# Attention scores as fp32 products on row halves of the array, decay and mask added on DVE

## The chip, the core and the metric

The kernel runs on one core of a Trainium2 chip. The core has TensorE (PE in the profile; its weight loads are PEld), the vector engine DVE, the scalar engine ACT, GpSimd (POOL), and SyncE (SP), whose queue starts the transfers. The metric is the device time of one execution in microseconds (us).

## The reference

Three parts follow one another: attention with a decay, a mixture of 8 experts whose gates are balanced by 8 rounds of scaling, and a two-layer part with a smooth activation. The change lies in the attention:

```python
scores = scale * np.matmul(q, k.transpose(0, 1, 3, 2))        # B=2, H=8, S=576, D=64
cum = np.cumsum(np.log(np.clip(f, 0.0001, 1.0)), axis=-1)
decay = cum[:, :, :, None] - cum[:, :, None, :]
scores = np.where(causal, -1000000000.0, scores + decay)
scores = scores - np.max(scores, axis=-1, keepdims=True)
attn = np.exp(scores)
attn = attn / (np.sum(attn, axis=-1, keepdims=True) + 1e-09)
return np.matmul(attn, v)
```

Its output x is the input of the experts (x @ w1, ReLU, @ w2, weighted by the gates), and theirs that of the last part.

## The kernel before

The order of all work is written out by hand, one loop of half steps `s`; each engine does its instructions in that order. Attention has ten query tiles, five a batch (`QT`: 128 queries, with one tile of 64 in each batch), with 128, 256, 384, 512 and 576 keys to look at. They are called tile 0 to tile 9 here; tiles 0 to 4 are batch 0, and tile 5 has the 64 queries of batch 1. A unit is a pair of heads of one tile, four units a tile, 40 in all; unit `pi` has the half steps `a` = 0 and 1, one for each of its heads.

A product of full precision is made from parts in the reduced type fp32r (FR): a value is a high part and a low part, each exact in that type. For the scores (`scores`, L361 on) the queries and keys of a tile are split into parts (`split`, L308, which calls `split2`, L284), turned by TensorE with head dimension on the partitions (`trans`, L321, 4 transposes a call, two calls each for queries and keys), and evacuated from PSUM by ACT or DVE, whichever the planner `pick` (L268) has given less time so far. `duplicate` (L300) copies half of the result by a transfer. A head's scores are two fp32r products that add up in PSUM: L374 with 128 rows, high and low query parts on the high key parts, and L375 with 96 rows, the missing product of parts and four rows that hold the decay (`cum_q`, `cum_k` load them). Scores of up to 512 keys are one group; 576 keys are two groups of 288. The mask pass on DVE (L387) adds a row of the mask, writes the negated scores and keeps their minimum; `expo` (L394) takes exponentials on ACT with their sums, one half step later; `normalize` (L402) multiplies by the reciprocal on POOL, `transposes` (L418) turns the weights in fp32, two units later, and `attend` (L444) multiplies them with v, three units later. In `attend` the two heads of a unit lie side by side on column halves of the array, 64 columns each; these are fp32 products.

Two other streams fill TensorE: `fill` (L535) takes the next piece of `filler` (L489), the first expert half on the tokens that are done, three products a piece, and `wsplit` (L565) splits its weights on ACT and DVE from unit 12 on. `warm` (L356) makes products without use that keep TensorE active in the first units. `gate` computes the gate logits of a chunk of 384 tokens. After the attention come the experts, from L695 on, with the same code in both kernels.

Of the kernel before, what the change touches and what calls it, by code (L numbers as in the profile page):

```python
# [8 lines left out]
F32 = mybir.dt.float32  # L9
# [74 lines left out]
def attention_moe_kernel(  # L84
# [46 lines left out]
    with ExitStack() as actx:  # L131
        ap1 = actx.enter_context(tc.tile_pool(name="ap1", bufs=1))
        rawp = actx.enter_context(tc.tile_pool(name="rawp", bufs=3))
        hlp = actx.enter_context(tc.tile_pool(name="hlp", bufs=2))
        kp = actx.enter_context(tc.tile_pool(name="kp", bufs=1))
        vp = actx.enter_context(tc.tile_pool(name="vp", bufs=6))
        pp = actx.enter_context(tc.tile_pool(name="pp", bufs=3))
        ptp = actx.enter_context(tc.tile_pool(name="ptp", bufs=2))
# [29 lines left out]
        cd = drp.tile([2, 16, S], F32, name="cd")  # L168


        KW = 832
        kbase = (256, 0)
        kt = kp.tile([128, H, KW], FR, name="kt")
        kbf = kp.tile([128, H, KW], FR, name="kb")
        kb = kbf[:96]
        qa = [kp.tile([128, 4, 128], FR, name=f"qa{i}") for i in range(3)]
        qb = [kp.tile([96, 4, 128], FR, name=f"qb{i}") for i in range(3)]

        def q_rows(i, engine=None):
            engine = engine or nc.gpsimd  # L180
            engine.memset(f(qb[i][64:96]), 0.0)
            engine.memset(f(qb[i][64:68]), -1.0)

        def k_rows(lo, hi, engine=None):
            (engine or nc.gpsimd).memset(f(kb[64:96, :, lo:hi]), 1.0)
# [17 lines left out]
        k_rows(256, 384, nc.vector)  # L203
        q_rows(0, nc.gpsimd)
        q_rows(1, nc.gpsimd)
        nc.vector.tensor_scalar(out=ft, in0=ft, scalar1=1e-4, scalar2=1.0, op0=ALU.max, op1=ALU.min)
        nc.vector.tensor_copy(out=idr, in_=idn)

        def cumulate(lo, hi, part=None):
            w = hi - lo  # L210
            if part != 1:
                cumulate_a(lo, hi, w)
            if part != 0:
                cumulate_b(lo, hi)

        def cumulate_a(lo, hi, w):
# [6 lines left out]
        def cumulate_b(lo, hi):  # L223
            nc.scalar.copy(out=chl[:, 0, lo:hi].bitcast(FR), in_=cum[:, lo:hi])
            nc.vector.tensor_tensor(
                out=chl[:, 1, lo:hi].bitcast(FR), in0=cum[:, lo:hi], in1=chl[:, 0, lo:hi], op=ALU.subtract
            )
            if lo == 0:
                for a in range(2):
# [1142 lines left out]
```

## Time and profile before

| | us |
|---|---|
| median of 3 runs | 1121.14 |
| lowest, highest | 1119.29, 1121.34 |
| span of the profiled execution, first to last instruction | 1123.8 |

The profiled execution has no time of its own beside its span; no run's time lies above it, so there is nothing around the span to add. Busy shares of its span are 99% for TensorE (with modelled ends), 76% for DVE, 45% for ACT and 7% for POOL. The engines' busy times are read by stretches below. "PEclk" is the granted share of TensorE's full clock: 1.0 is 2.4 GHz, 0.5 is 1.2 GHz, and a stretch with a value between had both.

### The profile page before, as it was taken

The page shows a single profiled execution, that of the slowest core. Times are in us where ns is not written, and L with a number is a line of the kernel's source. Part 1 is how long each engine was busy: PE and PEld are TensorE (multiplying, and loading weights), DVE is VectorE, ACT ScalarE, POOL GpSimd, SP SyncE. Part 2 cuts the span into 40 slices and gives each one's busy share as a digit, 9 for nine tenths or more (in the row PEclk, how much of TensorE's full clock was granted, in tenths as well). Part 3 has the DMA queues.
Part 4 walks back from the last instruction along what each step waited for, and adds up shares of the span by engine and source line. Part 5 has one row for each costly group of instructions (what it writes and reads, how often), then busy time and mean ns, then how long its engine had stood idle before and what let it go on. Part 6 is the DMA issues. An engine that isn't in the chain of part 4 may idle for free.

```text
span 1123.8 us, 17611 instructions
## 1 busy us (share of the span) xinstructions
PE 1109.8 (99%) x6608; PEld 981.3 (87%) x6608; DVE 852.3 (76%) x1850; ACT 504.3 (45%) x1128; POOL 76.7 (7%) x126
## 2 busy tenths in 40 slices
PE   8999999999999999999999999999999999999998
PEld 7677778989889898898988989899898988899996
DVE  7865655957786877868678686887868658998886
ACT  6766643245344253442534424243342335555554
POOL 5535420000000000000000000000000000000000
PEclk8899999999999999999999999999999999999999
DMA  5524212021332313323133241223311675000000
GB/s 124 145 65 105 53 39 76 20 75 42 128 110 77 124 50 130 105 75 132 49 113 110 86 140 58 94 96 111 122 67 57 205 253 198 1 29 1 29 1 29
DMA packets 78058, 98.93 MB, mean 88 GB/s; under 512 B 35190, under 2 KB 39046, under 8 KB 77974
## 3 DMA queue, kind: packets, MB, share of 16 engines
q1 hardware_dynamic: 77974, 97.81, 27.2%
q8 instruction: 52, 0.85, 0.3%
q14 instruction: 32, 0.26, 0.1%
HBM read 74.38 MB, written 19.21 MB: 83 GB/s over the span
## 4 chain that ended last, share of the span: by engine, by line
PE 93%; DVE 4%; ACT 1%; issue 1%; POOL 0%; DVEq 0%; ACTq 0%; POOLq 0%
PE pa L725 41%; PE pb L1080 28%; PE ph L695 11%; PE x L453 2%; PE pt L429 2%; PE pa L525 1%; PE sp L374 1%; PE ph L506 1%; PE pt L325 1%; DVE p L387 1%; PE sp L375 1%; PE x L862 0%; DVE r L973 0%; DVE r L967 0%; PE wt L359 0%
## 5 line engine op out<-in xcount | busy, mean ns | idle before, releaser
L725 PE MATMUL pa<-w2h,big 128*128 128x512 f32 x924 | 299.7, 393 | 1.2 <-DVE hid_b L703 1.2
L725 PEld LDWEIGHTS pa<-w2h,big 128*128 128x128 f32 x924 | 173.7, 188 | 39.7 <-DVE hid_b L703 1.5
L725 PE MATMUL pa<-w2l,big 128*128 128x512 f32 x528 | 207.2, 392 | 0.0
L1109 ACT COPY snap<-pb 128x288 f32<-128x288 f32 x168 | 66.4, 395 | 142.2 <-PE pb L1080 141.9
L725 PEld LDWEIGHTS pa<-w2l,big 128*128 128x128 f32 x528 | 99.3, 188 | 20.7
L703 DVE SCALAR_TENSOR_TENSOR big<-c,big 128x288 fp32r<-128x288 f32 x140 | 64.2, 459 | 69.4 <-ACT big L702 65.4
L702 ACT ACTIVATE big<-c 128x288 fp32r<-128x288 f32 x168 | 74.8, 445 | 91.8 <-DVE c L1114 89.0
L845 DVE SCALAR_TENSOR_TENSOR acc<-pa,P,acc 128x512 f32<-128x512 f32 x132 | 92.8, 746 | 27.2 <-PE pa L725 27.1
L1080 PE MATMUL pb<-xh,ss 128*128 128x288 f32 x448 | 103.9, 296 | 0.0
L1080 PE MATMUL pb<-tt,ss 128*128 128x288 f32 x672 | 103.7, 296 | 0.0
L1080 PEld LDWEIGHTS pb<-tt,ss 128*128 128x128 f32 x672 | 93.8, 188 | 1.0 <-ACT snap L1109 0.8
L1114 DVE TENSOR_TENSOR c<-pb,snap 128x288 f32<-128x288 f32 x168 | 75.9, 452 | 22.5 <-PE pb L1080 22.5
L824 ACT CAST db<-da 128x512 fp32r<-128x512 f32 x32 | 19.9, 621 | 147.8 <-DVE da L815 147.8
L1080 PEld LDWEIGHTS pb<-xh,ss 128*128 128x128 f32 x448 | 76.9, 188 | 0.6 <-DVE c L1114 0.3
L1080 PE MATMUL pb<-xl,ss 128*128 128x288 f32 x224 | 66.5, 297 | 0.0
L1080 PE MATMUL pb<-xh,w1l 128*128 128x288 f32 x224 | 66.2, 296 | 0.0
L1080 PE MATMUL pb<-xl,w1h 128*128 128x288 f32 x224 | 66.2, 295 | 0.0
L1080 PE MATMUL pb<-xh,w1h 128*128 128x288 f32 x224 | 66.1, 295 | 0.0
L725 PE MATMUL pa<-w2h,hid_b 128*128 128x512 f32 x150 | 58.6, 391 | 0.0
L397 ACT ACTIVATE p<-p,nmax 128x256 f32<-128x256 f32 (+6 forms) x80 | 48.4, 605 | 11.0 <-DVE nmax L387 8.4
L75 DVE TENSOR_TENSOR w2l<-stg,w2h 128x512 fp32r<-128x512 f32 x60 | 41.2, 690 | 15.9 <-ACT w2h L74 15.9
L413 POOL TENSOR_SCALAR p<-p,rs 128x256 f32<-128x256 f32 (+6 forms) x80 | 46.7, 596 | 66.4 <-DVE rs L409 42.2
(229 smaller groups left out, 2402.3 us busy)
## 6 DMA issues: line engine op xcount, KB each, us to landing
stg<-in_moe_w_dram SPq DMA_DIRECT2D x64, 512.0 KB
raw<-in_moe_w_in_dram SPq DMA_DIRECT2D x16, 512.0 KB
raw<-in_moe_w_out_dram SPq DMA_DIRECT2D x16, 512.0 KB
w_in_h<-db SPq DMA_DIRECT2D x16, 256.0 KB
w_in_l<-da SPq DMA_DIRECT2D x16, 256.0 KB
w_out_h<-db SPq DMA_DIRECT2D x16, 256.0 KB
w_out_l<-da SPq DMA_DIRECT2D x16, 256.0 KB
out_dram<-acc SPq DMA_DIRECT2D x9, 256.0 KB
```

What stands on the lines that cost most here:

```text
L75: (lo_engine or nc.vector).tensor_tensor(out=lo, in0=raw, in1=f(hi), op=ALU.subtract)
L397: nc.scalar.activation(out=p[:n, a, :nk], in_=p[:n, a, :nk], func=AF.Exp, bias=prev, scale=-1.0, accum_out=u["ssum"][:n, 0, a:a + 1],)
L413: nc.gpsimd.tensor_scalar(out=p[:n, a, :nk], in0=p[:n, a, :nk], scalar1=r[:n, a:a + 1], scalar2=1.0, op0=ALU.mult, op1=ALU.mult,)
L429: nc.tensor.transpose(out=pt[:, o + j * n:o + (j + 1) * n], in_=p[:n, a, j * 128:(j + 1) * 128], identity=idn[:n, :n],)
L695: nc.tensor.matmul(out=ph, lhsT=w[wn][kk][:, fs], rhs=x[c][:, kk], start=(kk == 0 and n == 0), stop=(kk == KD - 1 and n == 2),)
L702: nc.scalar.activation(out=hh, in_=ph, func=AF.Relu)
L703: nc.vector.scalar_tensor_tensor(out=hl, in0=ph, scalar=0.0, in1=f(hh), op0=ALU.max, op1=ALU.subtract)
L725: nc.tensor.matmul(out=pa, lhsT=a_[:, ts_], rhs=w[wn][ft_], start=(first and n == 0), stop=(last and n == 2),)
L845: nc.vector.scalar_tensor_tensor(out=acc[t], in0=pa, scalar=P[:, t, e:e + 1], in1=acc[t], op0=ALU.mult, op1=ALU.add)
L1080: nc.tensor.matmul(out=by_chunk(out_) if len(v_.shape) == 3 else out_, lhsT=u, rhs=v_, start=first and m == 0, stop=m == 5, skip_group_che ...
L1109: nc.scalar.copy(out=t, in_=bank["x", g])
L1114: nc.vector.tensor_tensor(out=t, in0=bank[of, g], in1=snap[with_, g], op=ALU.add)
```

## The change

Queries and keys stay unsplit in fp32. A transpose turns two heads at once, 64 rows of the array each (`turn`, 4 transposes for all 8 heads of queries or keys), so that a head's dimension lies on the upper or the lower 64 partitions. `scores` makes both heads of a unit together, at `a` = 0: a head is one fp32 product on its half of the array's rows; with 576 keys the last 64 or 128 keys are a further product each, in PSUM buffers of the transposes. The decay of the query is the same along a row and cancels, so it is left out; that of the keys is added on DVE, in fp32, by the pass that added the mask: `largest` has one pass over the keys before the tile's own (`bias`, loaded to all partitions by `load_bias`) and one over the tile's own keys (`diag`, loaded by `load_diag` and masked on POOL by `mask_diag`), the second continuing from the first one's minimum. For tile 0 that block comes from TensorE and DVE (`spread`). The products with v are made for two units at a time, at every second unit; `x_out` evacuates them. `duplicate`, `cum_q`, `cum_k`, the splits and their row fills are gone. The piece of `fill` moves from ahead of the products with v to the end of the half step. Two of the filler's hidden buffers come from the staging pool, whose buffers also take the expert weights. The diff, cut to its core:

```diff
-        rawp = actx.enter_context(tc.tile_pool(name="rawp", bufs=3))
-        hlp = actx.enter_context(tc.tile_pool(name="hlp", bufs=2))
+        rawp = actx.enter_context(tc.tile_pool(name="rawp", bufs=4))
         kp = actx.enter_context(tc.tile_pool(name="kp", bufs=1))
+        mdp = actx.enter_context(tc.tile_pool(name="mdp", bufs=2))
         vp = actx.enter_context(tc.tile_pool(name="vp", bufs=6))
         pp = actx.enter_context(tc.tile_pool(name="pp", bufs=3))
-        ptp = actx.enter_context(tc.tile_pool(name="ptp", bufs=2))
+        ptp = actx.enter_context(tc.tile_pool(name="ptp", bufs=3))
...
-        chl = pt0[1][:16, :, :S]
+        neg = pt0[1][:16, 0, :S]
         zer = ap1.tile([16, 1], F32, name="zer")
-        mask = ap1.tile([128, 704], F32, name="mask")
-
+        pick8 = ap1.tile([16, H, 128], F32, name="pick8")
+        mask = ap1.tile([128, 128], F32, name="mask")
...
+        cd = drp.tile([16, S], F32, name="cd")
+
+        KW = 704
+        kbase = (128, 0)
+        kt = kp.tile([128, 4, KW], F32, name="kt")
+        bias = kp.tile([128, H, KW], F32, name="bias")
+        hs1 = kp.tile([128, 12, 128], FR, name="hs1")
+        qt = [kp.tile([128, 4, 128], F32, name=f"qt{i}") for i in range(3)]
...
+        nc.gpsimd.memset(pick8, 0.0)
+        nc.gpsimd.affine_select(
+            out=pick8, in_=pick8, compare_op=ALU.not_equal, fill=-1.0, base=0,
+            pattern=[[-1, H], [0, 128]], channel_multiplier=1,
+        )
+        nc.gpsimd.memset(mask, 0.0)
+        nc.gpsimd.affine_select(
+            out=mask, in_=mask, compare_op=ALU.is_ge, fill=NEG, base=0,
+            pattern=[[-1, 128]], channel_multiplier=1,
...
+        def negate(lo, hi):
+            nc.scalar.mul(out=neg[:, lo:hi], in_=cum[:, lo:hi], mul=-1.0)
+            nc.sync.dma_start(out=cd[:, lo:hi], in_=neg[:, lo:hi])
+
+        def load_bias(b, lo, hi):
+            nc.sync.dma_start(
+                out=bias[:, :, kbase[b] + lo:kbase[b] + hi],
+                in_=cd[b * H:(b + 1) * H, lo:hi].partition_broadcast(128),
+            )
...
+        diag = {}
+
+        def span(b, i):
+            s0, n = QT[b][i]
+            return s0, min(S, -(-(s0 + n) // 128) * 128) - s0
+
+        def load_diag(ti):
+            b, i = tiles[ti]
+            s0, w = span(b, i)
+            diag[ti] = mdp.tile([128, H, 192], F32, tag="md", name="md")
+            nc.sync.dma_start(
+                out=diag[ti][:, :, :w], in_=cd[b * H:(b + 1) * H, s0:s0 + w].partition_broadcast(128)
+            )
+
+        def mask_diag(ti):
+            b, i = tiles[ti]
+            s0, w = span(b, i)
+            nc.gpsimd.affine_select(
+                out=diag[ti][:, :, :w], in_=diag[ti][:, :, :w], compare_op=ALU.is_ge, fill=NEG, base=0,
+                pattern=[[0, H], [-1, w]], channel_multiplier=1,
...
+        load_raw("q", q, 0, 128, 128)
+        load_raw("k", k, 0, 128, 128)
...
+        def turn(kind, ti, us=slice(0, 4)):
...
+            raw = raws[kind, b, s0]
+            pt = ps_t.tile([128, 4, 128], F32, tag="pt", name="pt")
+            for u in range(us.start, us.stop):
+                nc.tensor.transpose(
+                    out=pt[:, u, :n], in_=raw[:n, 2 * u:2 * u + 2].rearrange("p h d -> p (h d)"),
+                    identity=idn[:n, :n],
+                )
+            cols = (us.stop - us.start) * n
+            if kind == "q":
+                evac(qt[ti % 3][:, us, :n], pt[:, us, :n], cols, 0.125)
+            else:
+                o = kbase[b] + s0
+                evac(kt[:, us, o:o + n], pt[:, us, :n], cols)
...
-        def scores(u, a):
-            b, h, n, nk = u["b"], u["h"] + a, u["n"], u["nk"]
...
-            widths = [nk] if nk <= 512 else [nk // 2, nk // 2]
-            groups, o = [], 0
-            for w in widths:
...
+        def scores(u):
+            b, h, n, nk, s0 = u["b"], u["h"], u["n"], u["nk"], u["s0"]
+            k0, g = kbase[b], u["h"] // 2
+            lhs = [qt[u["ti"] % 3][64 * a:64 * a + 64, g, :n] for a in range(2)]
+            early = u["ti"] < 2 and g % 2
+            sp = [
+                (ps_f if early else ps_s).tile([128, 512], F32, tag="fb" if early else "s", name="sp")
+                for _ in range(2)
+            ]
+            rest = nk - s0 if nk > 512 else 0
+            if rest:
+                far = [ps_t.tile([128, 512], F32, tag="pt", name="far") for _ in range(2)]
+
+            def product(o, a, lo, hi):
+                nc.tensor.matmul(
+                    out=o, lhsT=lhs[a], rhs=kt[64 * a:64 * a + 64, g, k0 + lo:k0 + hi], start=True, stop=True
+                )
+
+            for a in range(2):
+                product(sp[a][:n, :nk - rest], a, 0, nk - rest)
+            if rest:
+                for a in range(2):
+                    product(far[a][:n, :rest], a, s0, nk)
+            u["p"] = pp.tile([128, 2, S], F32, tag="p", name="p")
+            u["ssum"] = sums4[(4 * u["ti"] + h // 2) % 4]
+            u["parts"] = []
+            for a in range(2):
+                parts = [(sp[a][:n, :s0], bias[:n, h + a, k0:k0 + s0], 0, s0)] if s0 else []
+                d = far[a][:n, :rest] if rest else sp[a][:n, s0:nk]
+                parts.append((d, diag[u["ti"]][:n, h + a, :nk - s0], s0, nk))
+                u["parts"].append(parts)
+
+        def largest(u, a):
+            n, p = u["n"], u["p"]
             prev = 3.0e38
-            for t, o, w in groups:
+            spent("dve", 110 + 67 + 1.05 * u["nk"])
+            for s_, t_, lo, hi in u["parts"][a]:
                 am = small.tile([128, 1], F32, tag="nmax", name="nmax")
                 nc.vector.tensor_tensor_reduce(
-                    out=p[:n, a, o:o + w], in0=t[:n, :w], in1=mask[:n, m0 + o:m0 + o + w],
-                    scale=-1.0, scalar=prev, op0=ALU.add, op1=ALU.min, accum_out=am[:n],
+                    out=p[:n, a, lo:hi], in0=s_, in1=t_, scale=-1.0, scalar=prev, op0=ALU.add, op1=ALU.min,
+                    accum_out=am[:n],
                 )
                 prev = am[:n]
             u["nmax", a] = prev
...
+        def x_out(u):
...
-                hs = []
-                for i in range(4):
-                    h0, c0 = 3 * (i % 2), 576 + 128 * (i // 2)
-                    hs.append(tuple(t[:, h0:h0 + 3, c0:c0 + 128] for t in (kt, kbf)))
+                hs = [tuple(hs1[:, 6 * i + 3 * j:6 * i + 3 * j + 3] for j in range(2)) for i in range(2)]
             for i in range(4):
+                if len(hs) == i:
+                    t = stage.tile([128, 2, 512], FR, tag="stg", name="spare")
+                    hs.append(tuple(t[:, j, :CH].rearrange("p (j t) -> p j t", j=3) for j in range(2)))
...
+        def spread(h0):
+            pb = ps_s.tile([128, 512], F32, tag="s", name="pb")
+            for h in range(4):
+                nc.tensor.matmul(
+                    out=pb[:, 128 * h:128 * h + 128], lhsT=pick8[:, h0 + h], rhs=cum[:, :128],
+                    start=True, stop=True,
+                )
+            nc.vector.tensor_tensor(
+                out=diag[0][:, h0:h0 + 4, :128], in0=pb.rearrange("p (h t) -> p h t", h=4),
+                in1=mask.unsqueeze(1).to_broadcast([128, 4, 128]), op=ALU.add,
+            )
+
+        def turn_half(g):
+            for kind in "qk":
+                turn(kind, 0, slice(2 * g, 2 * g + 2))
+
+        diag[0] = mdp.tile([128, H, 192], F32, tag="md", name="md")
+        cumulate(128, S)
         warm(8)
-        cumulate(128, S, 1)
+        turn_half(0)
+        spread(0)
         load_v(0, 0)
-        cum_k(0, 128, 256)
-
-        first = [
-            lambda: (qs0(1), ks0(1)), lambda: (qt0(1, True), kt0(1, True)),
-        ]
+        negate(0, S)
+        load_diag(1)
+        load_bias(0, 0, 128)
+        first = [lambda: spread(4), lambda: turn_half(1)]
...
             if live:
-                scores(units[pi], a)
+                if not a:
+                    scores(units[pi])
+                largest(units[pi], a)
             if s < 16:
                 warm(1)
-            fill()
-            if a and 3 <= pi < nu + 3:
-                w = units[pi - 3]
-                attend(w)
-                if w["h"] == H - 2 and w["ti"] in (2, 6, 9):
-                    c = (2, 6, 9).index(w["ti"])
-                    gates.append(c)
-                    if c < 2:
-                        fills.append(filler(c))
-                elif gates:
-                    logits.append(gate(gates.pop(0)))
-            elif logits:
+            if not a and pi % 2 == 0 and 4 <= pi < nu + 4:
+                for w in units[pi - 4:pi - 2]:
+                    attend(w)
+                if w["h"] == H - 2:
+                    x_out(w)
+                    if w["ti"] in (2, 6, 9):
+                        c = (2, 6, 9).index(w["ti"])
+                        gates.append(c)
+                        if c < 2:
+                            fills.append(filler(c))
+            elif a and gates:
...
                 if (st, a) == (0, 0):
-                    cum_q(nb_, ni, 0, (2 * ti + 2) % 3)
-                    qs()
+                    next_loads(ti + 2)
                 elif (st, a) == (0, 1):
-                    ks()
-                    next_loads(ti + 2)
-                elif (st, a) == (1, 0):
-                    qt_(0)
+                    turn("q", ti + 1)
                 elif (st, a) == (1, 1):
-                    kt_(0)
+                    turn("k", ti + 1)
                     load_v(nb_, ni)
-                elif (st, a) == (2, 0):
-                    qt_(1)
-                elif (st, a) == (2, 1):
-                    kt_(1)
-            if late_rows and s >= 2:
-                late_rows.pop(0)()
+                if (st, a) == (0, 1) and ti:
+                    load_diag(ti + 1)
+                    lo = [0, 0, 64, 192, 320][ni] if nb_ else 128 * max(ni - 1, 0)
+                    hi = [0, 64, 192, 320, 448][ni] if nb_ else 128 * ni
+                    if hi > lo:
+                        load_bias(nb_, lo, hi)
+                elif (st, a) == (3, 0):
+                    mask_diag(ti + 1)
+            fill()
```

## Rows read from the trace of the kernel before

**Rows 1.** Windows of attention and the rest: length, busy us (instructions) of engines, PEclk, DMA, GB/s.

```profile
0.00:178.00 178.00, 171.28 (x1346) 136.38 (x1346) 115.21 (x385) 112.11 (x287) 76.68 (x126) 0.94 0.37 87
178.00:1123.80 945.80, 938.52 (x5264) 844.92 (x5263) 737.12 (x1466) 392.23 (x841) 0.00 (x0) 1.00 0.26 88
```

**Rows 2.** Windows of the start, of tiles 0 to 3, and of tile 8.

```profile
core 0: us, PE busy (x) PEld busy (x) DVE busy (x) ACT busy (x) POOL busy (x), PEclk, DMA share, GB/s
0.00:9.50 9.50, 8.12 (x48) 7.93 (x48) 6.28 (x11) 4.23 (x9) 6.85 (x21) 1.00 0.32 72
9.50:21.80 12.30, 10.22 (x64) 9.22 (x64) 8.37 (x32) 9.64 (x28) 4.53 (x12) 0.72 0.76 161
21.80:31.40 9.60, 9.45 (x83) 7.88 (x82) 7.98 (x31) 8.16 (x26) 5.94 (x13) 1.00 0.63 142
31.40:42.00 10.60, 10.27 (x91) 7.79 (x89) 9.06 (x30) 8.73 (x23) 6.66 (x11) 1.00 0.80 203
42.00:64.80 22.80, 21.72 (x129) 15.76 (x128) 14.72 (x39) 12.57 (x33) 9.36 (x12) 0.70 0.34 88
...
124.40:142.00 17.60, 17.60 (x142) 14.45 (x141) 11.45 (x36) 12.16 (x30) 8.02 (x10) 1.00 0.23 55
```

**Rows 3.** The chain of waits by line, to 64.8 us and from there to 178.

```profile
by line: PE pt L429 11.4%; PE x L453 9.9%; PE sp L374 9.0%; PE pt L325 8.0%; PE sp L375 6.2%; PE wt L359 3.9%; issue 3.7%; DVE p L387 3.4%; PE ph L506 3.0%; DVE big L298 2.6%; ACT p L397 2.2%; DVE hl L288 2.1%; DVE hl L290 2.0%; POOL hl L29
...
by line: PE x L453 18.3%; PE pt L429 14.6%; PE pa L525 14.5%; PE ph L506 11.5%; PE sp L374 8.9%; DVE p L387 7.0%; PE sp L375 5.3%; PE pt L325 4.7%; issue 3.1%; DVE xl L460 1.5%; PE g L469 1.3%; PE g L474 1.2%; DVE qb L280 1.0%; PE pt L440 0
```

**Rows 4.** Timeline of TensorE's products: start us, duration us, line, tiles, shapes, count.

```profile
7.48 2.02 PE L359 MATMUL wt<-idn 128*128 128x128 f32 x16
...
21.27 0.44 PE L453 MATMUL x<-pT,v 128*64 128x128 f32 x4
...
42.57 0.39 PE L374 MATMUL sp<-kt,qa 128*128 128x512 f32 x1
42.80 0.39 PE L375 MATMUL sp<-kb,qb 96*128 96x512 f32 x1
43.12 0.88 PE L453 MATMUL x<-pT,v 128*64 128x128 f32 x12
43.93 0.88 PE L429 MATMUL pt<-idn,p 128*128 128x128 f32 x6
44.56 0.48 PE L374 MATMUL sp<-kt,qa 128*128 128x512 f32 x1
...
74.91 0.54 PE L325 MATMUL pt<-idr,hl 128*128 128x128 f32 x4
75.29 0.31 PE L374 MATMUL sp<-kt,qa 128*64 128x288 f32 x1
```

**Rows 5.** Groups by line and form in the attention: mask passes on DVE, an evacuation on ACT.

```profile
L387 DVE CUSTOM_DVE_ANT_0 p<-sp,mask 128x512 f32<-128x512 f32 x16 | 10.9, 685 | 7.0 <-PE sp L375 6.9
...
L387 DVE DVE_READ_ACCUMULATOR2_ANT nmax<- 128x1 f32 x72 | 5.9, 82 | 0.0
...
L387 DVE CUSTOM_DVE_ANT_0 p<-sp,mask 128x128 f32<-128x128 f32 x8 | 2.2, 280 | 0.5 <-PE sp L375 0.5
...
L276 ACT ACTIVATE qa<-pt 64x512 fp32r<-64x512 f32 x12 | 7.0, 586 | 5.7 <-PE pt L325 4.9 <-DVE qb L280 0.8
```

**Rows 6.** Groups by line on POOL in the attention.

```profile
L290 POOL TENSOR_TENSOR hl<-raw,hl 128x512 fp32r<-128x512 f32 (+1 forms) x14 | 18.4, 1315 | 13.5 <-PE sp L375 7.6 <-ACT hl L286 5.9
...
L242 POOL TENSOR_SCALAR_AFFINE_SELECT mask<-mask 128x704 f32<-128x704 f32 x1 | 0.8, 774 | 0.1
```

**Rows 7.** Timeline of the start, all engines.

```profile
4.29 0.70 ACT L318 CAST hl<-raw 128x256 fp32r<-128x256 f32 x2
...
9.54 0.30 PE L374 MATMUL sp<-kt,qa 128*128 128x128 f32 x1
...
11.04 0.27 DVE L387 CUSTOM_DVE_ANT_0 p<-sp,mask 128x128 f32<-128x128 f32 x1
```

**Rows 8.** Timeline in tile 3: POOL and DVE, and the next scores.

```profile
44.05 1.34 POOL L290 TENSOR_TENSOR hl<-raw,hl 64x512 fp32r<-64x512 f32 x1 [0.92 <-PE sp L375]
44.28 1.66 DVE L298 TENSOR_TENSOR big<-stg,big 128x512 fp32r<-128x512 f32 x1
46.85 0.51 PE L374 MATMUL sp<-kt,qa 128*128 128x512 f32 x1 [0.92 <-DVE nmax L387]
```

More of the change, by code (lines that the diff above doesn't have):

```diff
@@ L221, in cumulate_a @@
             )
[L223 to L226, printed above, removed]
-            )
-            if lo == 0:
-                for a in range(2):
-                    nc.sync.dma_start(
-                        out=f(kb[66 + a:67 + a, :, kbase[0]:kbase[0] + hi]), in_=chl[:H, a, :hi]
-                    )
-                    nc.sync.dma_start(out=f(qb[0][64 + a:65 + a, :, :hi]), in_=chl[:4, a, :hi])
-            nc.sync.dma_start(out=cd[:, :, lo:hi].rearrange("a p s -> p a s"), in_=chl[:, :, lo:hi])
@@ L236, in attention_moe_kernel @@
-        cumulate(0, 128)
-        early = stage.tile([128, 2, H, D], F32, tag="stg", name="early")
-        for a, (nm, src) in enumerate((("q", q), ("k", k))):
-            nc.sync.dma_start(out=early[:, a], in_=src[0, :, 128:256, :].rearrange("h p d -> p h d"))
-            raws[nm, 0, 128] = early[:, a]
-        nc.gpsimd.memset(mask, 0.0)
-        nc.gpsimd.affine_select(
-            out=mask, in_=mask, compare_op=ALU.is_ge, fill=NEG, base=512,
-            pattern=[[-1, 704]], channel_multiplier=1,
-        )
@@ L249, in attention_moe_kernel @@
+        cumulate(0, 128)
+        load_raw("q", q, 0, 128, 128)
+        load_raw("k", k, 0, 128, 128)
         for t in sums4:
             nc.gpsimd.memset(t, 1.0)
-        late_rows = [lambda o=o: k_rows(o, o + 64) for o in range(512, 832, 64)]
-        late_rows += [lambda: cum_k(0, 256, S)] + [lambda o=o: k_rows(o, o + 64) for o in range(0, 256, 64)]
+        nc.gpsimd.memset(ones, 1.0)
         busy["pool"] = 10000.0
-        def cum_k(b, lo, hi):
-            nc.sync.dma_start(
-                out=f(kb[66:68, :, kbase[b] + lo:kbase[b] + hi]), in_=cd[:, b * H:(b + 1) * H, lo:hi]
-            )
@@ L410, in normalize @@
             spent("dve", 350)
-            busy["pool"] += 2 * (90 + 1.1 * nk)
             for a in range(2):
@@ L548, in attention_moe_kernel @@
             nk = min(S, -(-(s0 + n) // 128) * 128)
-            slots = [(2 * ti) % 3, (2 * ti + 1) % 3]
             sh = {}
             for h in range(0, H, 2):
-                units.append(dict(b=b, i=i, h=h, slots=slots, s0=s0, n=n, nk=nk, tile=sh, ti=ti))
+                units.append(dict(b=b, i=i, h=h, s0=s0, n=n, nk=nk, tile=sh, ti=ti))
         def next_loads(ti):
@@ L587, in attention_moe_kernel @@
         nu = len(units)
-        for s in range(2 * nu + 8):
+        for s in range(2 * nu + 10):
             pi, a = divmod(s, 2)
```

146 lines of the change are left out of this document (16 added, 130 removed).

## The prediction

> **What bounds the kernel now.** The windows come first. Attention fills the first 178 us of 1123.8; the rest has the same code in both kernels [rows 1]. So only those 178 us are to be priced. By its modelled ends TensorE looks busy nearly all of them, while DVE is busy for 65% and ACT for 63%. The granted clock says more: 0.72 in query tile 0 and 0.70 in tile 3, full speed in tiles 1 and 2 and everywhere later [rows 2]. A mean of 0.70 over tile 3's 22.8 us is 13.7 us at the half level of 1.2 GHz. The chain of waits is read last: TensorE carries most of it, and the others that appear are short steps of DVE, ACT and POOL ahead of a product: mask passes (L387), splits of queries and keys (L288, L290), a weight split (L298) [rows 3]. After 64.8 us TensorE's own work is nearly the whole chain, and a change there counts by what TensorE has to do. Before 64.8 us it counts by what TensorE waits for.
>
> **Scores on TensorE.** The timeline of its products gives three prices [rows 4]. An fp32 product is two records here: 16 records stand for the 8 warming products. They took 2.02 us, the last one's 0.27 included, so one with 128 moving columns takes (2.02 - 0.27)/15 = 0.117 us: two passes at 2.4 GHz (0.107) and 0.01. A record of the fp32r scores over 512 keys takes 42.80 - 42.57 = 0.23 us, one pass at 2.4 GHz (0.213) and 0.017; I scale others so. A head has two, a pair of heads four (eight half as long with 576 keys). After the change a pair is two fp32 products of half the rows, four records of two passes. Whether row halves overlap no row of before shows. The nearest rows are the products with v, which lie on column halves: four of their records, two heads of one key block, took 0.44 us with the last one's 0.27, so the last began 0.17 after the first; one behind the other it would have been 0.35. The second record of one half runs with the first of the other, and a pair costs three record times instead of four. From below, a perfect pair costs two, from above four. I take three, since these rows are the same engine, type and order.
>
> Per pair, after against before: 128 keys the same, since four loads of 128 columns (0.105 each, as for the transposes below) bound both; 256 keys 0.67 against 0.48; 384 keys 0.99 against 0.72; 512 keys 1.31 against 0.92; 576 keys about 1.40 against 1.07; the one tile of 64 queries over 128 keys 0.35 against 0.26. Four pairs a tile and two tiles of each width: 4 x (2 x (0.19 + 0.27 + 0.39 + 0.33) + 0.09) = +9.8 us.
>
> **Other work on TensorE.** Turning queries and keys takes 8 transposes a tile in place of 16. Four of the old ones took 75.29 - 74.91 = 0.38 us, six fp32 ones 44.56 - 43.93 = 0.63 us: 80 x 0.105 - 160 x 0.095 = -6.8 us. The first tile's decay comes from 8 small fp32 products, 16 records of 0.117: +1.9 us. A run of 12 records of the v products took 0.81 us from its start to the next transposes, where 12 x 0.053 (a pair of records in 0.107) is 0.64: 0.17 is lost when the array goes from halves back to whole, and up to 0.1 when it enters, 0.13 a turn. Before there are 40 such runs, 80 turns. After, 40 runs of row halves and 20 of two units' v products, 20 of them adjacent, make 100: +2.6 us. The Trainium skill's "TensorEngine Tiling (Array Packing)" (Tiling Modes, Key Properties) speaks against the change here: going from one tiling mode to another drains the engine. It has no price for it; by the row the 20 more turns cost 2.6 us, by the rule alone the sign is the same and the size open. Sum on TensorE: +7.5 us.
>
> **DVE, ACT, POOL.** A tile loses four of six evacuations (0.59 each on ACT) and the splits of its queries and keys, a high part on ACT or DVE and a low part mostly on POOL (1.3). It gains a second mask pass for each head where the row of keys has an off-diagonal part: passes of 512 and 128 columns take 0.685 and 0.280, so an extra one costs 0.145 and 0.08 for reading its minimum, 48 times, 10.8 us [rows 5]. Eight heads of a tile give +1.8 us against -2.4 for the evacuations and two or more for the splits: ACT and DVE together become lighter, by 10 x 2.4 - 10.8 = 13 us over the attention before the splits are counted. POOL loses 14 low parts of 1.3 and its row fills and gains nine masks of up to 1536 columns; 704 columns took 0.77, so at most 1.7 each, 11 in all [rows 6]. These stand on POOL ahead of a normalization, which TensorE's transposes need only a unit later, 2.4 us or more: free if the diagonal's load has landed.
>
> **Transfers.** A tile gains a diagonal block of 0.5 to 0.8 MB and a bias block of at most 0.5 MB, and loses four copies of together 0.5 MB. Tile 2 moved 203 GB/s at a share of 0.80 [rows 2], so full speed is some 254 GB/s and the added 0.5 to 0.8 MB take 2 to 3 us a tile, asked for two and a half units before POOL masks them. I cost them at nothing; in tiles 1 and 2, where little of the transfer time is free, a late diagonal would cost at most those 2 to 3 us each, kept for the range. On SP's queue the copies, which wait for evacuations, give way to loads that wait for nothing late. At the end the first weights of the next stage wait until two staging buffers used as spare hidden tiles are read; they land some 5 us later under the next layer's first products (2 us each): nothing, or 1 to 2 us if that cover is too short.
>
> **The stages.** *Start.* The first queries are there at 4.29, when ACT begins their split; the first scores begin at 9.54 and the first mask pass at 11.04 [rows 7]. After, 4 transposes follow at once (about 5.6), an evacuation of half a tile (to about 6.2), 8 records of the spread at the half clock (0.21 each, to 7.3), then the scores: -2.2 us. *Tile 0*, 12.3 us: its units wait for splits and evacuations of its second half and of tile 1. Tile 1's units, with twice the keys, take 2.4 us each under the same kind of load. I take 2.25: 9.0, -3.3 us. *Tiles 1 and 2*: TensorE +0.6 to +1 us each, its waits less by as much: 0. *Tile 3*, 22.8 us: the clock fell after a stretch in which a weight split on DVE took 1.66 us while POOL ran a low part beside it, and scores waited behind it [rows 8]. Tile 8 has the same keys, fills in all units, and took 17.6 us at full clock [rows 2]. DVE's 14.7 us in tile 3 stay about that (+1.8 for extra passes, as much less for evacuations and splits) and with gaps of 0.4 a unit make 4.1 us a unit: 16.5, -6.3 us, if the clock stays up. *From tile 4 on*, 113.2 us: of the sum on TensorE, scores +6.4, turns +1.6, transposes -3.4: +4.6. The chain there has 7% of mask passes, some 8 us, and 3 us of two other steps of DVE [rows 3]; I let the lighter engines take two fifths of these 11: -4.4. Sum 0.
>
> -2.2 - 3.3 - 6.3 = -11.8 us. The profiled execution's span, which has nothing of weight around it, is 1123.8 us, 0.24% above the runs' median of 1121.14. The sum gives 1112.0 for that execution and 1109.3 for the median; I say 1109.
>
> **Rivals.** *Row halves do not overlap:* four record times. That adds one a unit: 8 x (0.22 + 0.33 + 0.44 + 0.42) = 11.3 us, of which perhaps 2 hide under other waits: 1109 + 9 to 11, 1119. The v products speak against it, on the other side of the array. Chance 0.13. *A pair needs both banks (slower):* both heads' scores are now issued together into two buffers, so the next unit's second product waits for the second head's mask pass, which stands on DVE behind the fill's low part or an evacuation. In a unit without enough work between, TensorE waits. This decides from 11.8/40 = 0.3 us a unit; if a whole mask pass of 0.69 is exposed in each of the 40 it is +27 us: 1136; if it is half, 1123. For it: scores already wait for these minima in the chain. Against: transposes, v products and fills, 2.4 us or more, lie between. Chance 0.14. *The clock falls again in tile 3:* half of 13.7 us at full speed is lost again: -6.3 is gone, 1115. Chance 0.12. *A perfect pair:* two record times, 11.3 us less on TensorE, of which some 8 show: 1101. The Trainium skill's "TensorE: Matmul & The Clock Gate" (Part 3, Measured speedup vs the span model) has tiles in one array take one product's time and 4 ns for each further tile; by that rule it is 1101, but it is told of single-record products, and the v products' 0.44 us say three. Chance 0.06.
>
> **How the numbers follow.** The forecast holds 0.55: 1109, by itself 1103 to 1117. A measurement of this kernel tells some 0.2%, 2.2 us, from no change. Forecast, clock and perfect pair are faster, with half of the first rival: 0.78, less 0.02 for the tails, 0.76. The other half and the bank rival's small values: 0.10 the same. Slower 0.14. The range leaves out the slow half of the bank rival, and the fast end of the perfect pair: 1100 to 1123.
>
> **What would show it.** Right: scores as record pairs that begin together, three record times from first to next work; the first mask pass near 8.3 us; a clock of 1.0 in tile 3 and that tile at 16 to 17 us; tiles 4 to 9 within 3 us of before; two mask passes a head at 0.2 more. Wrong: four score records one behind the other; scores waiting for minima in every unit; POOL's masks waiting for their transfers; the first products of the next layer waiting for weights.

## The result, and the profile after

The change makes the kernel slower: 1131.45 us (median of four, 1128.79 to 1132.22) against 1121.24; ratio 1.0088, 95% interval 1.0069 to 1.0107. 1109 was predicted. The profiled execution has a span of 1127.0 us and is the fastest of its four runs. Its time is 1128.79, 1.8 us above its span; in every other run that has both it is 1.7 to 1.9. So there is something around the span after all, and the profiled execution of before, with a span of 1123.8, took some 1125.6 us (an estimate), 0.4% above its median.

The windows of the changed kernel, against [rows 2]: the start, tiles 0 to 3, tile 8.

```profile
core 0: us, PE busy (x) PEld busy (x) DVE busy (x) ACT busy (x) POOL busy (x), PEclk, DMA share, GB/s
0.00:6.70 6.70, 5.30 (x28) 5.04 (x28) 3.17 (x5) 3.00 (x5) 3.78 (x16) 1.00 0.65 147
6.70:21.20 14.50, 13.17 (x57) 10.34 (x56) 5.13 (x25) 4.87 (x18) 3.22 (x7) 0.65 0.89 188
21.20:35.00 13.80, 11.33 (x69) 7.61 (x68) 7.39 (x42) 7.66 (x24) 4.56 (x9) 0.91 0.78 195
35.00:47.40 12.40, 11.49 (x78) 6.88 (x77) 8.61 (x42) 7.59 (x21) 4.79 (x10) 0.96 0.62 139
47.40:66.40 19.00, 17.95 (x125) 11.07 (x124) 12.70 (x49) 11.59 (x29) 5.53 (x9) 1.00 0.28 78
129.80:146.50 16.70, 16.70 (x125) 11.72 (x124) 11.48 (x47) 10.58 (x27) 6.21 (x10) 1.00 0.28 71
```

The start is 2.8 us shorter. Tiles 0, 1 and 2 are 2.2, 4.2 and 1.8 longer, with the clock at 0.65 and DVE busy for 35% of tile 0. Tile 3 keeps its clock, but takes 19.0 us where 16.5 were forecast. Its chain to 66.4 us, against [rows 3]:

```profile
by line: PE sp L318 26.4%; PE wt L302 16.4%; PE pt L383 11.1%; PE x L407 9.4%; PE pt L286 8.5%; PE pb L523 4.5%; PE ph L462 3.8%; issue 3.3%; DVE p L342 3.2%; DVE xl L416 3.1%; ACT xh L415 2.7%; DVE md L527 1.1%; PE g L430 1.1%; PE g L425 1
```

Scores have gone from 15% of the chain (L374, L375) to 26%, warming products from 4% to 16%. TensorE's timeline where nothing disturbs it, against [rows 4], shows that this isn't the price of the products:

```profile
129.75 1.13 PE L318 MATMUL sp<-kt,qt 64*128 64x512 f32 x4
130.81 1.53 PE L407 MATMUL x<-pT,v 128*64 128x128 f32 x24
```

A pair of heads with 512 keys takes 1.06 us from its first record to the next work. Both heads' first records begin 0.01 us apart, the two second ones 0.53 later: the row halves overlap, and a pair costs two of the prediction's record times (0.44) and 0.2 more. DVE's mask passes, against [rows 5]:

```profile
L342 DVE DVE_READ_ACCUMULATOR2_ANT nmax<- 128x1 f32 x120 | 10.0, 83 | 0.0
L342 DVE CUSTOM_DVE_ANT_0 p<-sp,md,nmax 128x128 f32<-128x128 f32 x24 | 8.4, 351 | 1.2
...
L342 DVE CUSTOM_DVE_ANT_0 p<-sp,md 128x128 f32<-128x128 f32 x8 | 2.3, 288 | 4.6 <-PE sp L318 4.5 <-DVE md L527 0.2
```

### The profile page after: what moved, and what is told of

Read it like the earlier page. It is cut to its first block, busy times and chain, and to the rows that moved or that the text cites. A ratio compares the mean times of both kernels' runs of the same rounds, so it can differ in the third digit from the quotient of the medians.

```text
span 1127.0 us, 17323 instructions
## 1 busy us (share of the span) xinstructions
PE 1110.0 (98%) x6520; PEld 963.7 (86%) x6520; DVE 838.8 (74%) x1903; ACT 489.8 (43%) x1096; POOL 59.6 (5%) x107
## 4 chain that ended last, share of the span: by engine, by line
PE 95%; DVE 3%; ACT 1%; issue 0%; POOL 0%; DVEq 0%; POOLq 0%; ACTq 0%
PE pa L681 41%; PE pb L1036 28%; PE ph L651 11%; PE sp L318 3%; PE x L407 3%; PE pt L383 2%; PE ph L462 2%; PE pa L481 2%; PE wt L302 1%; PE pt L286 1%; DVE p L342 0%; PE x L818 0%; DVE r L929 0%; DVE xl L416 0%; ACT xh L415 0%
## 5 line engine op out<-in xcount | busy, mean ns | idle before, releaser
L1065 ACT COPY snap<-pb 128x288 f32<-128x288 f32 x168 | 66.4, 395 | 141.2 <-PE pb L1036 140.7
L352 ACT ACTIVATE p<-p,nmax 128x256 f32<-128x256 f32 (+6 forms) x80 | 48.4, 605 | 35.0 <-DVE nmax L342 18.1
L318 PE MATMUL sp<-kt,qt 64*128 64x256 f32 (+6 forms) x160 | 46.1, 516 | 5.0 <-DVE nmax L342 3.2
```

Source lines behind the costliest of these rows:

```text
L318: nc.tensor.matmul(out=o, lhsT=lhs[a], rhs=kt[64 * a:64 * a + 64, g, k0 + lo:k0 + hi], start=True, stop=True)
L352: nc.scalar.activation(out=p[:n, a, :nk], in_=p[:n, a, :nk], func=AF.Exp, bias=prev, scale=-1.0, accum_out=u["ssum"][:n, 0, a:a + 1],)
L1065: nc.scalar.copy(out=t, in_=bank["x", g])
```

## The experiments

Eighteen kernels ran, in six groups; the edits are shown shortened; each ratio is to the kernel before on the same chip. Stage times are read as in the windows, from the first score record of each tile; "to x" runs from tile 6 to the last product with v.

**The kernel before once more.** No edit.

> The kernel before, unchanged, profiled again. The profile on which the prediction rests has a span of 1123.8 us, above every timed run (1119.3 to 1122.0). Theory 'atypical profile': its half clock in tile 3 is not the rule; here tile 3 takes 17 to 19 us instead of 22.8, the span is 1117 to 1120, and the -6.3 us that the prediction took for tile 3 never were to be had. Rival 'typical profile': half clock in tile 3 again, span near 1123, and the loss of 10 us lies in the changed kernel alone. Time against before: 1.000 either way.

Measured: 1120.87 us, span 1117.5.

```profile
8.70:20.40 11.70, 9.18 (x66) 8.27 (x65) 8.37 (x32) 9.44 (x28) 4.37 (x11) 0.85 0.84 176
...
40.80:58.50 17.70, 16.28 (x130) 11.58 (x128) 14.48 (x39) 12.25 (x33) 9.31 (x12) 1.00 0.44 113
```

Tile 3 takes 17.7 us at full clock. The 22.8 of [rows 2] are not the usual case: of 102 timed runs of this kernel beside the experiments, 22 have a mean granted clock of 0.992 or less, as that profile has (0.991), and take 1122.4 to 1126.9 us; where in them the clock fell isn't recorded. In the usual execution tile 3 had nothing of the kind to give.

**Loads and mask passes.** The first leaves out the loads and POOL's masks on them, the second the 48 extra passes (its expectation says 40 of 48, but tiles with 576 keys had two passes before, so all 48 go); in both the decay is missing from scores. The third keeps all of the computation.

```diff
-parts = [(sp[a][:n, :s0], bias[:n, h + a, k0:k0 + s0], 0, s0)] if s0 else []   # e1_noload
+parts = [(sp[a][:n, :s0], mask[:n, :1].to_broadcast([n, s0]), 0, s0)] if s0 else []
+if s0 and not rest:                                                            # e2_onepass
+    parts = [(sp[a][:n, :nk], mask[:n, 512 - s0:512 - s0 + nk], 0, nk)]
-out=diag[ti][:, :, :w], in_=cd[b * H:(b + 1) * H, s0:s0 + w].partition_broadcast(128)   # e7_rowbias
+out=diag[ti][:, :, :s0 + w], in_=cd[b * H:(b + 1) * H, :s0 + w].partition_broadcast(128)
+parts = [(sp[a][:n, :nk - rest], diag[u["ti"]][:n, h + a, :nk - rest], 0, nk - rest)]
```

> The changed kernel without the loads of decay rows (load_bias, load_diag) and without POOL's masks on them; DVE adds a constant zero column and one constant triangle instead, so the decay is left out of the scores, the number and shape of all other instructions is the same. Theory 'transfers': the partition-broadcast loads hold up queries, keys, values and weights in tiles 0 to 2 and POOL's masks hold up normalizations; attention becomes 4 to 8 us shorter (1123 to 1127), tiles 1 and 2 by 2 to 4 us each. Theory 'passes' (DVE's 48 extra mask passes and the second head's pass standing late on DVE): no more than 2 us.

Measured: 1131.18 us, 1.0086 (1.0062 to 1.0109). Nothing: the loads are hidden here, and the theory of transfers falls for this kernel. (Its profiled execution ran at half clock until 20.9 us, but all four runs lie within 2.0 us.)

> The changed kernel with one mask pass a head, as before, where the keys are up to 512 (a constant triangle over all keys, so the decay is left out of these scores); the loads of decay rows and POOL's masks stay. Removes 40 of the 48 extra passes, about 9 us of DVE. Theory 'passes': TensorE's scores wait for these passes, 6 to 9 us shorter than after (1122 to 1125), most of it from tile 4 on. Theory 'transfers': -1 to -3 us, since the loads stay and only the wait for them goes. If the passes are hidden behind TensorE: 0 to -2.

Measured: 1123.86 us, 1.0029 (1.0018 to 1.0040): 7.6 us less. In the profiled executions tiles 1 to 3 are 4.3 us shorter and those from 4 on 1.4; the expectation had most of it from tile 4 on. Of the 4.3, some 1.6 go with half clock in tiles 1 and 2 of the changed kernel's profile: e8, below, has as much less there with all passes.

> The changed kernel with decay and mask of a tile in one buffer over all its keys (loaded whole for each tile, the diagonal part masked in place), so that the one mask pass a head of the kernel before is enough up to 512 keys and nothing of the computation is left out. The loads grow (keys 0 to the end of the tile again for each tile). Theory 'passes': as with one pass and a constant triangle, 6 to 8 us shorter than after, 1123 to 1125. If larger loads now come too late for POOL's mask: tiles 2 and 3 longer by 1 to 3 us, 1125 to 1128.

Measured: 1126.28 us, 1.0045 (1.0027 to 1.0063): 5.2 us less with the whole computation, short of the 6 to 8 forecast. Tiles 2 and 3 are not longer (11.0 and 18.1 us, as in e2), so it isn't late loads; its profile has 17.1 us at half clock after the first rise, the changed kernel's 13.7.

**Order of the work.** One part of the change each put back or moved.

```diff
-for w in units[pi - 4:pi - 2]:      # e3_xsingle: products with v, at a == 1
-    attend(w)
+attend(units[pi - 3])
-if not a:                           # e4_perhead
-    scores(units[pi])
+scores(units[pi], a)
-first = [lambda: spread(4), lambda: turn_half(1)]      # e5_start, spread(4) in ps_t
+first = [lambda: None, lambda: turn_half(1), lambda: None, lambda: spread(4)]
 if s < 16:                          # e6_fill: fill() here, not at the end of the half step
     warm(1)
+fill()
```

> The changed kernel with the products with v one unit at a time, at the place in the order that they have in the kernel before. 20 more runs of column halves, so 40 more turns: by the prediction's 0.13 us a turn +2.6 to +5 us on TensorE (1134 to 1137). Theory 'bunching': two units at once come later and put the copies of x out right in front of scores and fills, and keep DVE from mask passes; one at a time is 2 to 5 us shorter (1126 to 1129).

Measured: 1134.79 us, 1.0123 (1.0098 to 1.0148).

> The changed kernel with each head's score product issued in its own half step, as in the kernel before, so that a bank is asked for only when the other is being read, and the row halves of a pair never overlap. Theory 'both banks': a good part of the loss is the second head's product waiting for the mask pass of the unit before; then the loss of overlap (8 to 11 us by the prediction's prices) is paid back in part: 1127 to 1134. Theory 'no bank wait': nothing is paid back, 1139 to 1143. If the halves had not overlapped anyway: 1128 or less.

Measured: 1159.21 us, 1.0342 (1.0307 to 1.0377), outside both. TensorE ran at half clock from 8.2 to 52.6 us; at full clock, from tile 4 to the last product with v, it takes 126.3 us (79.5 to 205.9) for 110.6, 0.65 us a unit: the overlap and the turns that it spares are worth that.

> The changed kernel with the second half of tile 0's preparation moved: transposes of heads 4 to 7 one unit-half later in the list, the spread of their decay two half steps later and into another bank pool, so that DVE's sum of decay and mask no longer stands ahead of the second head's first mask pass and no score bank is lent to it. Theory 'order at the start': tile 0, 14.5 to 15.3 us after and 11.6 before, gets 2 to 3 us back, 1128 to 1129. Theory 'clock at the start': tile 0 is long because TensorE runs at 1.2 GHz there; order alone gives under 1 us.

Measured: 1132.66 us, 1.0112 (1.0081 to 1.0143), from 1126.64 to 1139.01.

> The changed kernel with fill() back at the place that it has in the kernel before: right behind the scores and mask pass, ahead of products with v and transposes. Theory 'fill': behind the transposes, its hidden tiles' relu and low part come late on ACT and DVE in front of the next mask pass: 1 to 3 us shorter. Rival: the place is free, within 1 us of after; tiles 0 to 2, which have no fill, stay as they are in any case.

Measured: 1138.13 us, 1.0155 (1.0099 to 1.0212), from 1131.43 to 1145.32. In each of the four profiled executions TensorE ran longer at half clock than in that of the changed kernel (e3 to 27.1 us and again at 37.3 to 44.1, e4 to 52.6, e5 to 37.7, e6 at 88 to 115), so their times say more of the clock than of the edit.

**The clock.** The kernel before makes 20 warming products ahead of its first scores, the changed one 8. (e10 is the kernel before with 8.)

```diff
-warm(8)          # e8_warm20
+warm(12)
 turn_half(0)
 spread(0)
+warm(8)
-warm(1)          # e9_warm4
+warm(4 if s < 8 else 2)
```

> The changed kernel with 20 warming products ahead of the first scores, as the kernel before has (12, the first transposes and the spread, 8), in place of 8. They delay the first scores by some 2.5 us (24 records of 0.11 to 0.21). Theory 'clock': with only 8 the TensorE clock falls back to 1.2 GHz at 8.6 us and stays there through tile 0 (after: 10.3 us of half clock in tiles 0 and 1, before: 3.4 us), which makes tiles 0 and 1 some 5 us longer; with 20 the clock stays up in tile 0, tile 0 takes 11 to 12.5 us instead of 14.5, tile 1 11 to 12, and the sum with the delay is -2 to -4 us. Theory 'waits' (tile 0 is long through DVE's order and waits): +2 us.

Measured: 1124.87 us (ten runs within 0.9 us), 1.0024 (1.0008 to 1.0041): 6.6 us less, more than the 2 to 4 forecast. Windows of tiles 0 to 2:

```profile
9.40:18.70 9.30, 8.22 (x57) 6.45 (x56) 4.38 (x24) 4.64 (x18) 2.52 (x6) 1.00 0.97 208
18.70:31.40 12.70, 10.23 (x71) 6.87 (x70) 7.39 (x42) 7.26 (x23) 5.19 (x11) 1.00 0.93 236
31.40:43.30 11.90, 10.99 (x77) 6.64 (x76) 8.59 (x42) 7.96 (x23) 4.83 (x11) 1.00 0.80 153
```

Scores begin 2.7 us later, and tile 0 takes 9.3 us in place of 14.5, near the 9.0 of the prediction. Between the two profiled executions the difference is 4.0 us: tile 0 -5.2, tiles 1 and 2 -1.6, start +2.7.

> The changed kernel with four warming products a half step in tile 0 and two in tile 1, instead of one. Theory 'clock': TensorE falls to 1.2 GHz because it stands still between units of tile 0; filled gaps keep the clock up, half clock under 5 us after the first scores, -2 to -4 us in spite of 28 more products (0.23 us each at full speed, 6.6 us, partly in gaps). If the gaps are too short for them, or the clock falls all the same: +3 to +8 us, since each costs 0.42 at half clock.

Measured: 1135.39 us, 1.0122 (1.0086 to 1.0158). The clock rose only at 17.8 us; tile 0 took 19.5. More products between units did not help.

> The kernel before without its first 12 warming products (8 remain, as in the changed kernel); nothing else differs. Theory 'clock': it falls to half clock in tiles 0 and 1 as the changed kernel does, and is 2 to 6 us slower than before. If the 12 products were only a delay, or TensorE's clock does not set the time of the first tiles: same or up to 1 us faster.

Measured: 1119.02 us, 0.9982 (0.9967 to 0.9996). The theory missed here: the old order brings the clock up by itself at 11.6 us and keeps it. The twelve products are needed by the new order alone; why it needs them isn't shown.

> Decay and mask of a tile in one buffer (one mask pass a head), together with the 20 warming products. If 'passes' and 'clock' are the two causes and add: 1126 less 2 to 4, 1122 to 1124, within 0.4% of before. If the clock is not a cause: 1128.

Measured: 1121.76 us, 1.0005 (0.9988 to 1.0021): 3.1 us below e8. Level with before.

**The same three parts with the clock up.** Edits as above, on e8; e15 is e11 with 16 warming products and the later second half of tile 0.

> 20 warming products, and the second half of tile 0's preparation moved behind as in the earlier run on the order of the start; to be held against 1124.87 us with 20 products alone. Theory 'order at the start': with the clock up, tile 0 goes from 9.3 to 8 to 8.5 us, 1124. Rival: with the clock up the order there costs nothing, 1124.5 to 1125.5.

Measured: 1130.23 us, 1.0074 (1.0052 to 1.0096): no gain. Half clock came back at 15.6 to 25.8 us; its runs go from 1124.99 at a mean clock of 0.999 to 1130.71 at 0.994. The slowest is the profiled one, with 13.7 us at half clock after the first rise, as much as the changed kernel's: one and the same kernel loses 5.7 us by the clock.

> 20 warming products, and fill() back at its place of before; to be held against 1124.87 us. In the earlier run the clock fell at 88 to 115 us, so 1138 tells little of the place. If the place is worth nothing: 1124 to 1126 and no half clock. If the order itself lets TensorE stand still in tiles 4 and 5 (and the clock then falls): half clock there again, 1130 or more. Tiles 0 to 2 the same in any case.

Measured: 1133.49 us, 1.0107 (1.0074 to 1.0140). Half clock at 79.7 to 89.9 us, in tiles 4 and 5, 23.8 us for 21.2 and 16.0 for 14.4; tiles 6 to 8 are 2.3 longer at full clock. The new place is worth keeping.

> 20 warming products, and the products with v one unit at a time; to be held against 1124.87 us. By the row of before (0.17 us lost at the end of a run, 0.1 at most at its start) 20 more runs cost 2.6 to 5.4 us on TensorE; tiles 6 to 9 show it best: 73 to 77 us in all for 73.1 to the last scores' work. If two at a time only shifts work: within 1 us.

Measured: 1127.05 us, 1.0057 (1.0041 to 1.0072). Two units at a time gain 2.2 us. The traces have 47 turns more in e14 (151 for 104), not 40, but also less waiting between the heads of a pair, as the theory of bunching in e3 had it: tiles 4 and 5 are 1.5 us shorter, tile 6 to x 1.6 longer. Of the 1.8 us between the two profiled spans only 0.3 lie between the first scores and the last product with v, so a price of a turn can't be read from the 2.2.

> One mask pass a head (decay and mask in one buffer), 8 warming products before and 8 behind the first transposes and the spread, and the later second half of tile 0. Held against 1121.76 us with 20 products. If 16 keep the clock up: scores begin 1 us earlier, 1120 to 1121, level with before or 0.1% faster. If the clock falls in tile 0: 1125 or more.

Measured: 1122.28 us, 1.0010 (0.9997 to 1.0024). No better than e11, and in neither range.

**The single warming products.** On e11: `if s < 16` becomes `if s < 8`, then the two lines go.

> One mask pass a head and 20 warming products at the start, without the eight single warming products of tile 1's half steps. Held against 1121.76 us. Theory 'they stand on the path': a product with its turn takes 0.33 us of TensorE, eight make 2.6; tile 1 from 11.7 to 9.5 to 10.5 us, 1119.5 to 1120.5. Rival 'they keep the clock up': half clock in tile 1 or 2, 1124 or more. If TensorE waits there anyway: within 0.5 us.

> As the run before, without the single warming products of tile 0 too. If those of tile 0 also stand on the path: another 0.5 to 1.5 us less, 1118.5 to 1119.5. If they are what keeps the clock up between tile 0's short units: half clock from tile 0 on, 1124 to 1130.

Measured: 1122.21 us, 0.9998 (0.9982 to 1.0014), and 1119.60 us, 0.9984 (0.9970 to 0.9998). In the profiled executions the clock stays up without them, but not in all runs of e16: five have a mean clock of 0.999 or more and take 1120.2 to 1120.7 us, six have 0.995 to 0.997 and take 1122.6 to 1124.1. Tile 1 goes from 11.7 to 8.2 us, tile 0 from 9.4 to 7.1. e17 is the fastest kernel of the new scheme, 0.16% below before, with an interval that ends just short of no change; the kernel before without its twelve warming products (e10) is as far below it. Most of what it wins is lost again in tiles 2 and 3:

```profile
16.70:25.10 8.40, 6.99 (x55) 4.18 (x54) 5.40 (x27) 6.57 (x22) 4.05 (x9) 1.00 1.15 287
25.10:37.90 12.80, 10.78 (x77) 6.45 (x76) 7.10 (x29) 8.15 (x23) 5.64 (x11) 1.00 1.05 279
37.90:58.40 20.50, 17.90 (x124) 10.72 (x123) 11.62 (x33) 11.56 (x29) 6.77 (x11) 1.00 0.64 183
```

Its timeline says to what, in square brackets the idle time and what ended it:

```profile
40.40 1.10 POOL L233 TENSOR_SCALAR_AFFINE_SELECT md<-md 128x1024 f32<-128x1024 f32 x1 [3.30 <-DMA md<-cd]
41.48 1.14 POOL L361 TENSOR_SCALAR p<-p,rs 128x384 f32<-128x384 f32 x2
41.53 0.69 DVE L336 CUSTOM_DVE_ANT_0 p<-sp,md 128x512 f32<-128x512 f32 x1 [2.94 <-POOL md L233]
...
42.12 1.11 PE L377 MATMUL pt<-idn,p 128*128 128x128 f32 x6 [1.60 <-POOL p L361]
```

The decay's load, 2 MB here, is now late; POOL waits for it ahead of a normalization, and TensorE's transposes with it. The loads that cost nothing in a slow kernel bound a fast one: the same load waits 0.3 us of POOL's time in e11 and 3.3 here. These loads are the larger ones of e7; the changed kernel's smaller ones weren't tried with so short a start.

## Why the prediction was wrong

The stages of the executions that carry the argument (us):

| | predicted | before | before again | after | e8 | e11 | e17 |
|---|---|---|---|---|---|---|---|
| start | 7.3 | 9.5 | 8.7 | 6.7 | 9.4 | 9.5 | 9.6 |
| tile 0 | 9.0 | 12.3 | 11.6 | 14.5 | 9.3 | 9.4 | 7.1 |
| tiles 1, 2 | 20.2 | 20.2 | 20.4 | 26.2 | 24.6 | 22.8 | 21.2 |
| tile 3 | 16.5 | 22.8 | 17.6 | 19.0 | 19.0 | 18.1 | 20.5 |
| tiles 4, 5 | | 32.5 | 32.5 | 35.6 | 35.6 | 35.1 | 35.1 |
| tile 6 to x | | 76.1 | 76.0 | 75.0 | 75.0 | 74.1 | 74.1 |

The sum gave 1112.0 for the profiled execution, and it measured 1127.0. By stages, after against forecast: start -0.6, tile 0 +5.5, tiles 1 and 2 +6.0, tile 3 +2.5, from tile 4 on +2.0, behind the attention -0.4.

**Tile 3, -6.3 us: failed.** It took half clock of a minority of executions for a cost of the kernel. The profiled span lay above the time of every timed run; the sum took the 0.24% between it and the median off all stages alike and did not ask which stage held it. By the 1.8 us between span and time it was 0.4%. Against a usual execution tile 3 loses 1.4 us.

**Tile 0, -3.3 us: failed by the clock.** With 8 warming products the clock falls at 8.6 us, or hasn't risen yet (e1, e2, e5, e9: at 17.8 to 37.7 us). That rival was placed in tile 3 alone. The cost is 6.6 us net of the later start. That tile 0 takes 9.3 us at full clock, near the 9.0, is in part luck: it holds staggered pairs (below) and single warming products that the sum didn't have, and without them e17 takes 7.1.

**Tiles 1 and 2, 0: failed; the bank rival is the mechanism.** TensorE's waits were to shrink by what its work grew; in their place came waits for PSUM banks. The rival was given 0.14, decides from 0.3 us a unit, and is there with 0.37 (e8). I add up, over 40 units, how much later a pair's last record begins than in an undisturbed pair of its width:

```
                    units staggered   sum us   tiles 0, 1   tiles 2, 3   from tile 4
e8  (clock up)            16           14.7        5.8          5.0          3.9
e11 (one pass)            13           10.7        4.9          3.3          2.5
e16 (no warm, tile 1)     11            8.3        2.0          3.8          2.5
e17 (no warm)              9            6.3        0.0          3.8          2.5
```

The sum fell by 4.0 from e8 to e11, the stretch from the first scores to the last product with v by 4.1 in these two traces, the median time by 3.1. The sum has two sources. In e8's timeline of tile 1 the second head's product stands two microseconds behind the first's:

```profile
27.40 0.69 DVE L416 TENSOR_TENSOR xl<-x,xh 128x512 fp32r<-128x512 f32 x1 [0.41 <-ACT xh L415]
...
27.52 0.70 PE L318 MATMUL sp<-kt,qt 64*128 64x256 f32 x2
...
28.27 0.27 DVE L342 CUSTOM_DVE_ANT_0 p<-sp,bias 128x128 f32<-128x128 f32 x1
...
28.59 0.35 DVE L342 CUSTOM_DVE_ANT_0 p<-sp,md,nmax 128x128 f32<-128x128 f32 x1
...
29.20 0.35 DVE L342 CUSTOM_DVE_ANT_0 p<-sp,md,nmax 128x128 f32<-128x128 f32 x1
...
29.47 0.08 DVE L342 DVE_READ_ACCUMULATOR2_ANT nmax<- 128x1 f32 x1
...
29.70 0.67 PE L318 MATMUL sp<-kt,qt 64*128 64x256 f32 x2 [1.48 <-DVE nmax L342]
```

DVE comes to the mask passes only after the low part of x (27.40) and the reciprocals, does two heads' four passes in order, and the read at 29.47 lets the product go. Here the wait is for the first head's own passes: in tiles 0 and 1 every second unit takes its banks from `ps_f`, which has two, one of them that of the warming products. Only those units are staggered there, and in e16 and e17 exactly those of tile 1, then of both tiles, are not any more. The trace has the second product wait for a read of the first head's own minimum, which the code allows for a shared bank alone; moving the warming products to another bank wasn't tried. The second source, from tile 2 on, is the one that the prediction named: two banks, both wanted at once, the second free only after the mask pass of the unit before. "Transposes, v products and fills lie between" held for 31 of 40 units in e17; at 34.9 us, for one, the low part of x stood ahead of the passes on DVE again, and the second head began 1.4 us late.

**Extra mask passes, 10.8 us of DVE, hidden: mis-sized and not hidden.** DVE's passes and reads rise from 53.6 to 68.4 us, 0.31 for each of 48: one that starts from a running minimum takes 0.351 us at 128 columns, one without 0.288. DVE as a whole did become lighter, 115.2 [rows 1] to 102.6 us; that said nothing, because the passes stand between a product and its bank. They cost 3.1 us with the clock up (e8 to e11), 5.2 with half clock at the start (after to e7).

**Scores on TensorE, +9.8: mis-sized.** A free pair costs two record times and 0.2, near the rival of the perfect pair: 0.42, 0.63, 0.85, 1.06 and 1.12 to 1.17 us by width, +4.4 in all. The row of before was misread: in the trace behind its four v records they begin at 21.268, 21.274, 21.428 and 21.434, two and two together, not one behind the other; the price of 0.053 that the prediction itself takes for a record in the run of 12 says the same. The rule of the Trainium skill's "TensorE: Matmul & The Clock Gate" (Measured speedup vs the span model), one product's time and a few nanoseconds for the other tile, fits the starts of these records (0.01 us apart); the 0.2 is beside it. The perfect pair's 1101 did not come, since the pairs that wait eat more than it saves.

**Turns, 0.13 each: open.** From e8 to e14 the stretch from the first scores to the last product with v grows by 0.3 us while the staggered sum falls from 14.7 to 10.7; if both count in full, the 47 turns cost some 0.09 each (an estimate). **Transfers at nothing: right** in the changed kernel (e1), wrong in a faster one (e17). **Start, -2.2:** -2.0 against a usual execution; first scores at 6.72, first mask pass at 7.74. **From tile 4 on, 0:** +3.1 in tiles 4 and 5, -1.0 after, with 3.9 us of staggered pairs in these six tiles.

Together: clock 6.6 and passes 3.1 of the 10.4 us between 1131.45 and 1121.03 (before, beside e8 and e11); the rest, 0.7, is within what the medians can tell.

## What to carry to other kernels

Time the kernel again, or at least hold the profiled span against the runs, before a stage with an odd clock goes into a sum. Hold a price against every row that shows the same thing. Two products issued side by side need two free banks at the same moment: follow each bank to the instruction that frees it and count what stands ahead of that on its engine, however idle the engine is. When a start is made leaner, its clock has to be looked after anew, and loads that a slow stage hides have to be priced for the fast one.

## What had not been expected of the hardware

The clock of a window is only as good as its first record. In the run without loads, the window of tile 0 and the warming products in it:

```profile
8.00:23.20 15.20, 14.17 (x57) 11.04 (x56) 5.13 (x25) 4.86 (x18) 2.15 (x6) 1.00 0.61 119
```

```profile
19.41 1.22 PE L301 MATMUL wt<-idn 128*128 128x128 f32 x4
```

The same four records took 0.71 us in e8 at 14.12. The column says 1.00, but the trace's first clock record is at 20.9 us, and until then records follow each other at 0.213 us, the half level. Read the spacing of equal products instead. That first rise came between 4.6 and 7.2 us in all nine traces with 24 warming records at the start; in the new order with 16 there it came at 4.8 to 6.6 us in six traces and at 17.8 to 37.7 in four (e1, e2, e5, e9). What decides it isn't settled by these runs.
